# Seven products in the up layers, attention ahead, and a planned order, in an attention and two-layer kernel

## The chip, the cores and the metric

The kernel runs on one core of a Trainium2 chip. The metric is the time of one execution in microseconds, as the device takes it. PE is TensorE (matmuls), DVE is VectorE, ACT ScalarE, POOL GpSimd, SP SyncE, which here issues the DMAs.

## The reference, cut to what matters

Batch 2, 8 heads, 768 positions, head size 64; 1536 tokens of width 512; each layer goes to 2048 and back.

```python
for b in range(nb):                       # attention, by blocks of positions
    intra = np.einsum('bhic,bhjc->bhij', qb, kb) * Dmask[None]
    intra = np.einsum('bhij,bhjd->bhid', intra, vb)
    inter = np.einsum('bhid,bhde->bhie', qb * lam_pow[None], kv_state)
    out[:, :, sl] = intra + inter
    kv_state = lam_block[None, :, None, None] * kv_state + np.einsum('bhsd,bhse->bhde', kb_dec, vb)
x = attn_out.transpose(0, 2, 1, 3).reshape(1536, 512)
h = x @ w_in                              # layer 1: ELU
x = np.where(h > 0.0, h, np.exp(np.minimum(h, 0.0)) - 1.0) @ w_out
h = x @ moe2_w_in                         # layer 2: a slope of its own for each of 2048 columns
out = (np.maximum(h, 0.0) + alpha * np.minimum(h, 0.0)) @ moe2_w_out
```

## The kernel before

Every layer operand is held as two float32r tiles, a high half (a rounded copy, ACT) and a low half (the rest, a subtraction on POOL or DVE), and every product is three matmuls: high by high, high by low, low by high. The weights arrive as 64-bit words; `split_w` makes them float32 by one ACT pass (L125) and three DVE passes (L126, L128, L131) over 128x1024 tiles, and then splits them (L134 on ACT, L135 on POOL).

The tokens lie in three chunks of 512. An item is one chunk and one tile of 128 of the 2048 ff columns: `up` does twelve matmuls of 128x512 into a PSUM bank, ACT and DVE make `g` of it (L373 to L381), ACT and POOL split it (L383, L384), and two items later `down` does twelve matmuls. The four down sums of a chunk stay in PSUM for a group of four ff tiles, and then `flush` copies them to `acc` or adds them to it (L416). There are 96 items; the order is layer, group, chunk, ff tile.

Attention has twelve blocks of 128 positions. A block's work on PE is `state` (L223), `scores` of the next block (L201) and `outputs` (L256, L262); DVE masks the scores (L208), adds the state (L241) and takes the low half of the output (L275). Four blocks (`AHEAD`) run before the first item, the other eight each beside an item. The blocks of the second batch follow those of the first.

The order of every engine is that of the program. Work that belongs to a later place is put off by `later(n, step)`, which runs it after n ticks; a tick comes after every three up matmuls and after each down group. The numbers of ticks are written by hand (`gaps`, `first`, `early`, `when`). In `begin` the first weight load stands on the SP queue between the loads of the second and the third block. PSUM's eight banks are taken in turn by all.

Of the kernel before, what the change touches and what calls it, by code (L numbers as in the profile page):

```python
# [1 line left out]

# [20 lines left out]
NCH = NT // CH  # L23
NCC = DM // 128
NF = DFF // 128
NPAIR = NF // 2
NG = 4
GF = NF // NG
LAG = 2
AHEAD = 4  # L30
# [3 lines left out]
def attention_two_layers(  # L34
# [14 lines left out]
    PSUM = bass.MemoryType.PSUM  # L49


    tiny = ctx.enter_context(tc.tile_pool(name="tiny", bufs=1))
    const = ctx.enter_context(tc.tile_pool(name="const", bufs=1))
    wraw = ctx.enter_context(tc.tile_pool(name="wraw", bufs=3))
    wt = ctx.enter_context(tc.tile_pool(name="wt", bufs=2))

    wsp = ctx.enter_context(tc.tile_pool(name="wsp", bufs=3))

    accp = ctx.enter_context(tc.tile_pool(name="accp", bufs=4))
    small = ctx.enter_context(tc.tile_pool(name="small", bufs=2))  # L60
    tmp = ctx.enter_context(tc.tile_pool(name="tmp", bufs=2))
    gp = ctx.enter_context(tc.tile_pool(name="gp", bufs=LAG + 2))
    ps = ctx.enter_context(tc.tile_pool(name="ps", bufs=8, space=PSUM))

    def bank(name):
        return ps.tile([128, 512], F32, tag="ps", name=name)

    alpha_sb = tiny.tile([128, NF], F32, name="alpha_sb")
    beta = tiny.tile([128, NF], F32, name="beta")
    warm = tiny.tile([128, C], F32, name="warm")  # L70
    anti = tiny.tile([128, C], F32, name="anti")
    lam_sb = tiny.tile([128, H], F32, name="lam_sb")
    lamp = tiny.tile([128, H], F32, name="lamp")
    row = tiny.tile([1, 128 + H], F32, name="row")
    fill = tiny.tile([128, 40], F32, name="fill")


    clock = [0]
    due = {}

    def later(n, step):
        if n:
            due.setdefault(clock[0] + n, []).append(step)
        else:
            step()

    def tick():
        clock[0] += 1
        for step in due.pop(clock[0], []):
            step()  # L90
# [3 lines left out]
    raw = {}  # L94
    split = {}

    def load_w(c):
        n, part = divmod(c, 2)
        l, k = divmod(n, NPAIR)
        wi, wo = wts[l]  # L100
        r = wraw.tile([128, 2048], U32, tag="raw", name="raw")
        if part == 0:
            nc.sync.dma_start(
                out=r.rearrange("p (c f) -> p c f", c=NCC),
                in_=wi[:, k * 512:(k + 1) * 512].rearrange("(c p) f -> p c f", p=128))
        else:
            nc.sync.dma_start(
                out=r.rearrange("p (f e) -> p f e", f=2),
                in_=wo[k * 256:(k + 1) * 256, :].rearrange("(f p) e -> p f e", p=128))
        raw[c] = r  # L110

    def split_w(c, gaps=(5, 6, 8, 11, 13), first=3):
        n, part = divmod(c, 2)
        r = raw.pop(c).rearrange("p (f w) -> p f w", w=2)


        upper, lower = r[:, :, 1], r[:, :, 0]
        t = wt.tile([128, 1024], F32, tag="wt", name="wt")
        tu = t.bitcast(U32)
        tag = "wi" if part == 0 else "wo"  # L120
        h = wsp.tile([128, 1024], F32R, tag=tag + "h", name=tag + "h")
        lo = wsp.tile([128, 1024], F32R, tag=tag + "l", name=tag + "l")
        shape = dict(c=NCC) if part == 0 else dict(c=2)
        split[c] = [x.rearrange("p (c f) -> p c f", **shape) for x in (h, lo)]
        later(first, lambda: nc.scalar.mul(t, upper.bitcast(F32), 2.0 ** -112))  # L125
        later(gaps[0], lambda: nc.vector.tensor_scalar(  # L126
            out=tu, in0=tu, scalar1=3, scalar2=None, op0=ALU.logical_shift_left))
        later(gaps[1], lambda: nc.vector.scalar_tensor_tensor(  # L128
            out=tu, in0=lower, scalar=29, in1=tu,
            op0=ALU.logical_shift_right, op1=ALU.bitwise_or))  # L130
        later(gaps[2], lambda: nc.vector.scalar_tensor_tensor(  # L131
            out=tu, in0=upper, scalar=0x80000000, in1=tu,
            op0=ALU.bitwise_and, op1=ALU.bitwise_or))
        later(gaps[3], lambda: nc.scalar.copy(h, t))  # L134
        later(gaps[4], lambda: nc.gpsimd.tensor_tensor(  # L135
            out=lo, in0=t, in1=h.bitcast(F32), op=ALU.subtract))

    xh = {}
    xl = {}

    def new_x(t, nm):
        xh[t] = const.tile([128, NCC, CH], F32R, tag=f"xh{t}", name=f"{nm}h{t}")
        xl[t] = const.tile([128, NCC, CH], F32R, tag=f"xl{t}", name=f"{nm}l{t}")


    qp = small.tile([128, NP, C], F32, name="qp", bufs=1)
    lamc = qp[:, :, C - 1:C]
    dm = wsp.tile([128, 1024], F32, tag="wih", name="dm").rearrange(
        "p (s a i) -> p s a i", s=2, a=NP)

    rev = dm.rearrange("p s a i -> p a s i")[:, :, :, C - 1:C]
    sms = [wsp.tile([128, 1024], F32, tag=tag, name="sm").rearrange(
        "p (s a i) -> p s a i", s=2, a=NP) for tag in ("wil", "woh")]
    st2 = wsp.tile([128, 1024], F32, tag="wol", name="st").rearrange(
        "p (s a i) -> p s a i", s=2, a=NP)
    st = [st2[:, 0], st2[:, 1]]

    ld = {}
    vs = {}

    def load(n):


        t = accp.tile([128, 4, 512], F32, tag="acc", name="blk")
        z = t[:, 0:2].rearrange("p s (a i) -> p s a i", a=NP)
        nc.sync.dma_start(out=z, in_=kqT[n])
        m = 2 if n % PB != PB - 1 else 1
        u = t[:, 2:4].rearrange("p s (h d) -> p s h d", h=H)
        nc.sync.dma_start(
            out=u[:, 0:m], in_=vk[n, :, 0:m, :].rearrange("j a (h d) -> j a h d", h=H))  # L170
        ld[n] = z
        vs[n] = (u[:, 0], u[:, 1] if m > 1 else None)

    kd = {}
    qs = {}

    def scale(n):
        q_ = ld[n][:, 1]
        kk = vs[n][1]
        if kk is not None:  # L180
            kd_ = small.tile([128, H, D], F32, tag="kd", name="kd_t")
            nc.gpsimd.tensor_tensor(
                out=kd_.rearrange("p (a s) d -> p a s d", s=2),
                in0=kk.rearrange("p (a s) d -> p a s d", s=2),
                in1=rev.to_broadcast([128, NP, 2, D]), op=ALU.mult)
            kd[n] = kd_
        if n % PB:
            qs_ = small.tile([128, NP, C], F32, tag="qs", name="qs_t")
            nc.gpsimd.tensor_tensor(out=qs_, in0=q_, in1=qp, op=ALU.mult)
            qs[n] = qs_  # L190

    sc = {}

    def scores(n):
        z = ld[n]

        ps_ = [bank("sc"), bank("sc")]
        for pr in range(NP):
            for hs in range(2):
                a, b = hs * 64, (hs + 1) * 64  # L200
                nc.tensor.matmul(  # L201
                    out=ps_[hs][:, pr * C:(pr + 1) * C], lhsT=z[a:b, 0, pr, :],
                    rhs=z[a:b, 1, pr, :], start=True, stop=True)
        sc[n] = ps_

    def mask(n):
        for hs, p_ in enumerate(sc.pop(n)):
            nc.vector.tensor_tensor(  # L208
                out=sms[n % 2][:, hs], in0=p_.rearrange("p (a i) -> p a i", a=NP),
                in1=dm[:, hs], op=ALU.mult)  # L210

    cur = [0]

    def state(n):
        if n not in kd:
            return None
        kd_ = kd.pop(n)
        v_ = vs[n][0]
        p_ = bank("stp")
        for pr in range(NP):  # L220
            for hs in range(2):
                h = 2 * pr + hs
                nc.tensor.matmul(  # L223
                    out=p_[hs * 64:(hs + 1) * 64, pr * D:(pr + 1) * D], lhsT=kd_[:, h, :],
                    rhs=v_[:, h, :], start=pr == 0, stop=True, skip_group_check=True)
        return p_[:, 0:NP * D].rearrange("p (a d) -> p a d", a=NP)

    def new_state(n, p_):
        if p_ is None:
            return  # L230
        first = n % PB == 0
        old, new = st[cur[0]], st[1 - cur[0]]
        if not first:
            for pr in range(NP):
                nc.scalar.mul(new[:, pr, :], old[:, pr, :], lamc[:, pr, :])  # L235
        for hs in range(2):
            a, b = hs * 64, (hs + 1) * 64
            if first:
                nc.vector.tensor_copy(new[a:b, :, a:b], p_[a:b])
# [28 lines left out]
    def keep(n, po):  # L268
        t, o = divmod(n * C, CH)
        if o == 0:  # L270
            new_x(t, "x")
# [18 lines left out]
    def block_b(n, p_):  # L290
# [3 lines left out]
        if n + 4 < NBLK:  # L294
            load(n + 4)
# [246 lines left out]
```

## Time and profile before

| | |
|---|---|
| runs | 585.53, 585.78 (median), 586.66 us |
| profiled execution | span 584.1 us, from its first to its last instruction; its own time outside the span is not listed |
| instructions | 7319, of which PE has 2960 matmuls |
| DMA | 49.23 MB, mean 84 GB/s |

A span is the time between two instructions of one execution; the runs also hold what lies around it. The profile gives each engine's busy time, the chain of work that ended last, waits and who ended them, and a timeline of instructions.

### The profile page before, as it was taken

To read this page: it belongs to the slowest core of one execution; us is meant where nothing else is said; L and a number is where in the kernel's file an instruction comes from. 1 tells how busy PE (TensorE), PEld (TensorE's weight loads), DVE (VectorE), ACT (ScalarE), POOL (GpSimd) and SP (SyncE) were. 2 spreads that over 40 slices of the span, in tenths; PEclk is the share of its full clock that TensorE was granted. 3 is DMA by queue.
4 is the path that set the end of the run, shared out by engine and by line. 5 is a ranking of instruction groups with operands and counts; after the bars stand their busy time and mean duration, and the time that the engine had idled before them with its cause. 6 is when DMAs were issued, how large, how long until landed. Compare 5 with 4: busy or idle time off the path is not lost.

```text
span 584.1 us, 7319 instructions
## 1 busy us (share of the span) xinstructions
PE 575.3 (98%) x2960; PEld 475.6 (81%) x2960; DVE 271.8 (47%) x363; ACT 240.9 (41%) x374; POOL 227.9 (39%) x156
## 2 busy tenths in 40 slices
PE   7999999999999999999999999999999999999997
PEld 6886788888888888888888888888888888888886
DVE  7777444753534542543645731443553551641332
ACT  2536354565435444544654442533324323432220
POOL 3756512454324344344233444434415334432221
PEclk9999999999999999999999999999999999999999
DMA  8985300342202122122102212222204110000111
GB/s 323 412 329 172 101 1 6 140 143 73 73 0 85 60 73 72 73 72 73 53 20 81 68 69 73 72 74 72 73 0 141 31 46 0 2 0 1 72 73 72
DMA packets 18307, 49.23 MB, mean 84 GB/s; under 512 B 1250, under 2 KB 1506, under 8 KB 18274
## 3 DMA queue, kind: packets, MB, share of 16 engines
q1 hardware_dynamic: 18274, 48.77, 23.7%
q8 instruction: 23, 0.38, 0.3%
q14 instruction: 10, 0.08, 0.0%
HBM read 45.62 MB, written 3.15 MB: 83 GB/s over the span
## 4 chain that ended last, share of the span: by engine, by line
PE 93%; DVE 2%; DMA 2%; ACT 1%; POOL 0%; issue 0%; SPq 0%; DVEq 0%
PE dn L400 44%; PE up L362 43%; DMA raw<-in_w1i 2%; PE sc L201 1%; PE po L256 1%; PE po L262 1%; PE warm L281 1%; DVE wt L128 1%; PE stp L223 1%; ACT st L235 0%; DVE acc L416 0%; DVE wt L131 0%; POOL wol L135 0%; DVE st L241 0%; DVE wt L126 0%
## 5 line engine op out<-in xcount | busy, mean ns | idle before, releaser
L384 POOL TENSOR_TENSOR gl_t<-g_t,gh_t 128x512 fp32r<-128x512 f32 x96 | 125.1, 1304 | 320.4 <-ACT gh_t L383 265.9
L373 ACT ACTIVATE r_t<-up 128x512 f32<-128x512 f32 x96 | 57.3, 597 | 187.2 <-PE up L362 187.2
L383 ACT CAST gh_t<-g_t 128x512 fp32r<-128x512 f32 x96 | 59.6, 621 | 110.9 <-DVE g_t L377 57.9
L416 DVE TENSOR_TENSOR acc<-dn,acc 128x512 f32<-128x512 f32 (+1 forms) x73 | 46.9, 676 | 75.7 <-PE dn L400 75.7
L400 PE MATMUL dn<-gh_t,wol 128*128 128x512 f32 x192 | 74.9, 390 | 1.3 <-POOL wol L135 1.3
L381 DVE SCALAR_TENSOR_TENSOR g_t<-r_t,beta,up 128x512 f32<-128x512 f32 x48 | 35.7, 743 | 86.2 <-ACT r_t L373 77.5
L400 PE MATMUL dn<-woh,gl_t 128*128 128x512 f32 (+1 forms) x196 | 75.4, 385 | 0.0
L400 PE MATMUL dn<-woh,gh_t 128*128 128x512 f32 (+1 forms) x196 | 75.4, 385 | 0.0
L400 PE MATMUL dn<-wol,gh_t 128*128 128x512 f32 (+1 forms) x196 | 75.4, 385 | 0.0
L400 PE MATMUL dn<-gh_t,woh 128*128 128x512 f32 x192 | 75.3, 392 | 0.0
L400 PE MATMUL dn<-gl_t,woh 128*128 128x512 f32 x192 | 74.8, 389 | 0.0
L377 DVE SCALAR_TENSOR_TENSOR g_t<-r_t,up 128x512 f32<-128x512 f32 x48 | 32.8, 683 | 63.0 <-ACT r_t L376 63.0
L362 PE MATMUL up<-xh,wih 128*128 128x512 f32 x192 | 52.2, 394 | 0.0
L362 PE MATMUL up<-xl,wih 128*128 128x512 f32 x192 | 51.4, 389 | 0.0
L362 PE MATMUL up<-xh,wil 128*128 128x512 f32 x192 | 51.4, 389 | 0.0
L362 PE MATMUL up<-yh,wih 128*128 128x512 f32 x192 | 51.3, 389 | 0.0
L362 PE MATMUL up<-yl,wih 128*128 128x512 f32 x192 | 51.3, 389 | 0.0
L362 PE MATMUL up<-yh,wil 128*128 128x512 f32 x192 | 51.3, 389 | 0.0
L126 DVE TENSOR_SCALAR wt<-wt 128x1024 uint32<-128x1024 uint32 x32 | 29.7, 927 | 33.5 <-ACT wt L125 33.5
L400 PEld LDWEIGHTS dn<-gh_t,wol 128*128 128x128 f32 x192 | 36.0, 188 | 9.2 <-POOL wol L135 1.7
L400 PEld LDWEIGHTS dn<-woh,gl_t 128*128 128x128 f32 x196 | 36.8, 188 | 7.4
L400 PEld LDWEIGHTS dn<-wol,gh_t 128*128 128x128 f32 x196 | 36.8, 188 | 7.4
(57 smaller groups left out, 796.2 us busy)
## 6 DMA issues: line engine op xcount, KB each, us to landing
raw<-in_w1i SPq DMA_DIRECT2D x8, 1024.0 KB, 5.6
raw<-in_w1o SPq DMA_DIRECT2D x8, 1024.0 KB, 4.8
raw<-in_w2i SPq DMA_DIRECT2D x8, 1024.0 KB, 5.4
raw<-in_w2o SPq DMA_DIRECT2D x8, 1024.0 KB, 4.9
blk<-in_kqT SPq DMA_DIRECT2D x12, 512.0 KB, 6.9
blk<-in_vk SPq DMA_DIRECT2D x10, 512.0 KB, 8.2
out<-acc SPq DMA_DIRECT2D x11, 256.0 KB, 2.1
blk<-in_vk SPq DMA_DIRECT2D x2, 256.0 KB, 6.4
```

Of the source, the lines that this page charges most:

```text
L126: later(gaps[0], lambda: nc.vector.tensor_scalar(out=tu, in0=tu, scalar1=3, scalar2=None, op0=ALU.logical_shift_left))
L128: later(gaps[1], lambda: nc.vector.scalar_tensor_tensor(out=tu, in0=lower, scalar=29, in1=tu, op0=ALU.logical_shift_right, op1=ALU.bitwise ...
L201: nc.tensor.matmul(out=ps_[hs][:, pr * C:(pr + 1) * C], lhsT=z[a:b, 0, pr, :], rhs=z[a:b, 1, pr, :], start=True, stop=True)
L223: nc.tensor.matmul(out=p_[hs * 64:(hs + 1) * 64, pr * D:(pr + 1) * D], lhsT=kd_[:, h, :], rhs=v_[:, h, :], start=pr == 0, stop=True, skip_ ...
L362: nc.tensor.matmul(out=p_, lhsT=w[:, cc, fo:fo + 128], rhs=x[t][:, cc, :], start=n == 0, stop=n == 3 * NCC - 1)
L373: nc.scalar.activation(r, p_, AF.Relu, scale=-1.0)
L377: later(1, lambda: nc.vector.scalar_tensor_tensor(out=g, in0=r, scalar=-1.0, in1=p_, op0=ALU.add, op1=ALU.max))
L381: later(1, lambda: nc.vector.scalar_tensor_tensor(out=g, in0=r, scalar=beta[:, f:f + 1], in1=p_, op0=ALU.mult, op1=ALU.add))
L383: later(2, lambda: nc.scalar.copy(gh_, g))
L384: later(3, lambda: nc.gpsimd.tensor_tensor(out=gl_, in0=g, in1=gh_.bitcast(F32), op=ALU.subtract))
L400: nc.tensor.matmul(out=p_, lhsT=a, rhs=b, start=first and n == 0, stop=last and n == 2)
L416: nc.vector.tensor_tensor(out=a, in0=p_, in1=a, op=ALU.add)
```

## The change

Chunk 0 keeps its plain up products (`plain`). For chunks 1 and 2 and a pair of ff tiles the up product is a 2 by 2 block product (two ff tiles, two halves of the 512 inputs, two chunks of tokens), done as Strassen's seven products in Winograd's form (`PRODUCTS`, `seven`). The weight sums S1 to S4 are made for each pair (`weights`, `sums`), the token sums T1 to T4 once a layer (`combine`), in place in the `acc` tiles of chunks 1 and 2. Three partial results are copied out of PSUM (`kept`), three are added to them on DVE (`tile`), one goes to its nonlinearity from PSUM.

A down sum now takes only one pair of ff tiles in PSUM (six matmuls); every pair's is added to `acc`. The PSUM banks are given out by use: 0 to 2 to the seven products, 3 and 4 to plain ones, 5 to 7 to down sums.

All twelve attention blocks run before the layers, the two batches in turn (`ORDER`); the state is updated in place. The first weight loads wait for the outputs of the blocks in places 2 and 5 (`W0`, `W1`), and no weight load stands among the first block loads.

`build` states each operation with its cost per engine, what it reads and what it writes, and PE's order. `Plan.run`, a list scheduler that runs while the program is written, then gives each other engine its order: of what is ready, what PE needs first. It may give an operation to ACT or DVE, or to DVE or POOL, and keeps operations marked `shared` of DVE and POOL apart in its plan. On the chip the engines run in that order and wait for one another as before.

The core of the diff; of the removed lines only the items and the PSUM groups of before are shown.

```diff
+ORDER = [b * PB + k for k in range(PB) for b in range(B)]
+CHUNK = [[0, 6, 1, 7], [2, 3, 4, 5], [8, 9, 10, 11]]
...
+    def add(self, costs, run, reads=(), writes=(), late=0.0, shared=False):
+        op = Op(costs, run, late, shared)
+        for b in reads:
+            op.after.update(b.wrote)
+        for b in writes:
+            op.after.update(b.read or b.wrote)
+        for b in reads:
+            b.read.append(op)
+        for b in writes:
+            b.wrote, b.read = [op], []
+        op.after.discard(op)
+        self.ops.append(op)
+        return op
...
+                held = []
+                while ready[e]:
+                    item = heapq.heappop(ready[e])
+                    op = item[2]
+                    if op.begun:
+                        continue
+                    if op.shared and e in port and port[self.OTHER[e]] > now + 1e-9:
+                        held.append(item)
+                        continue
+                    if e == "POOL" and any(
+                            x.shared and not x.begun and x is not op and x.need < op.need
+                            and x.need + shift < now + op.costs[e] + self.HOLD for _, _, x in ready["DVE"]):
+                        held.append(item)
+                        continue
+                    slow = op.costs[e] - op.least
+                    slack = op.need + shift - now
+                    if slow > 0.3 and slack < slow or (
+                            e == "DVE" and "POOL" in op.costs and slack > self.SPARE) or (
+                            e == "DVE" and "ACT" in op.costs and slack > self.EASE):
+                        held.append(item)
+                        continue
+                    begin(e, op)
+                    break
+                for item in held:
+                    heapq.heappush(ready[e], item)
...
+def act(n, psum=False):
+    return ((172 if psum else 224) + n) / 1200
+def vec(n):
+    return (140 + n) / 960
+def vec2(n):
+    return (150 + n / 2) / 960
+def pool(n):
+    return 0.2 + n * 0.00214
...
+    def sub(dst, a, b, reads, writes, n, engines=("DVE", "POOL"), alu=ALU.subtract):
+        costs = {"DVE": vec(n), "POOL": pool(n)}
+        op({e: costs[e] for e in engines},
+           lambda e: on(e).tensor_tensor(out=dst(), in0=a(), in1=b(), op=alu),
+           reads, writes, shared=True)
...
+        eng = ("DVE", "POOL")
+        sub(lambda: s1, lambda: a21, lambda: a22, [b_t], [b_y], 256, eng, ALU.add)
+        sub(lambda: s3, lambda: a11, lambda: a21, [b_t, b_y], [b_y], 256, eng)
+        sub(lambda: s2, lambda: s1, lambda: a11, [b_t, b_y], [b_y], 256, eng)
+        sub(lambda: s4, lambda: a12, lambda: s2, [b_t, b_y], [b_y], 256, eng)
+        held[l, j] = y, b_y
...
+            p11, p21, p12, p22 = (place(raw1, 0), place(raw1, 1), place(raw2, 0), place(raw2, 1))
+            q11, q21, q12, q22 = (bufs(raw1, 0), bufs(raw1, 1), bufs(raw2, 0), bufs(raw2, 1))
+            if l:
+                parts("B11", p11, q11)
+            sub(p11, p12, p11, q11 + q12, q11, 2 * n)
+            parts("T1", p11, q11)
+            if l:
+                parts("B22", p22, q22)
+            sub(p12, p22, p12, q12 + q22, q12, 2 * n)
+            sub(p22, p22, p11, q11 + q22, q22, 2 * n)
+            parts("T2", p22, q22)
+            parts("T3", p12, q12)
+            if l:
+                parts("B21", p21, q21)
+            sub(p21, p21, p22, q21 + q22, q21, 2 * n)
+            parts("T4", p21, q21)
...
+    W0, W1 = 2, 5
...
+    PRODUCTS = [
+        ("A11", "B11", 0, 1, 0), ("A12", "B21", 1, 1, 1), ("S1", "T1", 2, 1, 0),
+        ("S2", "T2", 0, 0, 0), ("S4", "B22", 2, 0, 1), ("S3", "T3", 0, 0, 0),
+        ("A22", "T4", 0, 0, 1)]
...
+    def seven(l, j):
+        s = j % 2
+        for n, (a, b, k, opens, closes) in enumerate(PRODUCTS):
+            k = (k + j) % 3
+            def run(a=a, b=b, k=k, opens=opens, closes=closes):
+                i = 0
+                for w, x in ((0, 0), (0, 1), (1, 0)):
+                    for cc in range(2):
+                        nc.tensor.matmul(
+                            out=banks[k], lhsT=left(s, a, w)[:, cc, :],
+                            rhs=quad(b, x)[:, cc, :], start=bool(opens and i == 0),
+                            stop=bool(closes and i == 5), skip_group_check=True)
+                        i += 1
+            reads = [b_quad[b, p, o] for p in range(2) for o in range(2)]
+            reads += b_wa[s] if a[0] == "A" else b_ws
+            yield pe(6 * MM, run, reads, [b_ps[k]])
+            def kept(u, k=k):
+                copy(lambda: ut(u), lambda: banks[k], [b_ps[k]], [b_ut[u]], 512, True)
+            def tile(u, q, t, k=k):
+                op({"DVE": vec(512)}, lambda e: nc.vector.tensor_tensor(
+                    out=ut(u), in0=banks[k], in1=ut(u), op=ALU.add),
+                   [b_ps[k], b_ut[u]], [b_ut[u]])
+                finish(l, 2 * j + q, lambda: ut(u), b_ut[u], (l, j, q, t), False)
+            if b == "B11":
+                kept(0)
+            elif b == "B21":
+                tile(0, 0, 1)
+            elif b == "T1":
+                kept(1)
+            elif b == "T2":
+                kept(2)
+            elif b == "B22":
+                tile(2, 0, 2)
+            elif b == "T3":
+                tile(1, 1, 2)
+            else:
+                finish(l, 2 * j + 1, lambda k=k: banks[k], b_ps[k], (l, j, 1, 1), True)
...
+        for c in range(parts):
+            k = 5 + turn("dn", 3)
+            cols = slice(c * w, (c + 1) * w)
+            p_ = banks[k][:, 0:w]
+            def run(cols=cols, p_=p_):
+                i = 0
+                for q in range(2):
+                    g = gt(gslot[l, j, q, t])
+                    for a, x in ((0, 0), (0, 1), (1, 0)):
+                        if l == 0:
+                            lhs, rhs = wd(s, a)[:, q, e * 128:(e + 1) * 128], g[:, x]
+                        else:
+                            lhs, rhs = g[:, x, e * 128:(e + 1) * 128], wd(s, a)[:, q, cols]
+                        nc.tensor.matmul(
+                            out=p_, lhsT=lhs, rhs=rhs, start=i == 0, stop=i == 5)
+                        i += 1
+            reads = [b_g[gslot[l, j, q, t]] for q in range(2)] + b_wd[s]
+            yield pe(6 * MM / parts, run, reads, [b_ps[k]])
...
+            if j == 0:
+                copy(a, lambda p_=p_: p_, [b_ps[k]], b_a, 512, True)
+            else:
+                op({"DVE": vec(w)}, lambda _, a=a, p_=p_: nc.vector.tensor_tensor(
+                    out=a(), in0=p_, in1=a(), op=ALU.add), [b_ps[k], *b_a], b_a)
...
+    T0 = [(0, e) for e in range(4)]
+    T12 = [(t, e) for t in (2, 1) for e in range(4)]
+    E12 = [(t, e) for e in range(4) for t in (2, 1)]
...
+        for i in range(4):
+            block_load(i)
         scores(0)
         scale(0)
         scale(1)
+        for i in range(NBLK):
+            k = state(i)
+            if i + 1 < NBLK:
+                scores(i + 1)
+            outputs(i)
+            new_state(i, k)
+            if i + 4 < NBLK:
+                block_load(i + 4)
+            if i + 2 < NBLK:
+                scale(i + 2)
+            if i == 5:
+                b_raw[0].wrote, b_raw[1].wrote = [last[W0]], [last[W1]]
+                weights(0, 0)
+                sums(0, 0)
+                weights_down(0, 0)
...
+        for l in range(2):
             if l == 0:
+                merge(plain(0, 0))
+                weights(0, 1)
+                weights_down(0, 1)
+                merge(plain(0, 1))
+                merge(seven(0, 0), downs(0, 0, T0))
             else:
+                merge((), downs(1, 0, T0))
+                merge(seven(1, 0), downs(1, 1, T0))
+            sums(l, 1)
+            for j in range(1, NU - 1):
+                merge(chain(seven(l, j), at_once(weights, l, j + 1), at_once(sums, l, j + 1),
+                            plain(l, j + 1)),
+                      chain(*([downs(l, j, T0), downs(l, j - 1, T12)] if (l, j) == (0, 1) else
+                              [downs(l, j - 1, T12)]), at_once(weights_down, l, j + 1),
+                            downs(l, j, T0) if j > 1 else ()))
+            j = NU - 1
+            merge(seven(l, j), chain(downs(l, j, T0), downs(l, j - 1, T12)))
+            if l == 1:
+                merge((), downs(1, j, T12))
...
+            weights(1, 0)
+            sums(1, 0)
+            weights_down(1, 0)
+            weights(1, 1)
+            merge(chain(plain(1, 0), plain(1, 1)), downs(0, j, E12))
+            raw = [(acc[t], {(e, q): b_acc[t, e, q] for e in range(4) for q in range(2)})
+                   for t in (1, 2)]
+            combine(1, 1, *raw)
+            weights_down(1, 1)
...
-    items = [(l, q, t, q * GF + j)
-             for l in range(2) for q in range(NG) for t in range(NCH) for j in range(GF)]
-    PER = NCH * GF
...
-        if first:
-            dn[e, c0] = bank("dn")[:, 0:c1 - c0]
```

## Rows read from the trace of the kernel before

**Rows 1.** The page: engine, busy us, share, instructions.

```profile
PE 575.3 (98%) x2960; PEld 475.6 (81%) x2960; DVE 271.8 (47%) x363; ACT 240.9 (41%) x374; POOL 227.9 (39%) x156
```

**Rows 2.** The chain in time: start us, us, what.

```profile
98.80 2.72 PE dn L400 x12
...
316.40 2.72 PE dn L400 x12
```

**Rows 3.** Waits of PE: total us, times, longest us.

```profile
PE sc L201 <- DMA blk<-in_kqT: 2.3, 1, 2.3
PE dn L400 <- POOL wol L135: 1.3, 1, 1.3
...
PE po L262 <- DVE st L241: 0.5, 1, 0.5
```

**Rows 4.** Windows: busy us by engine, PE clock, DMA share, GB/s.

```profile
10.00:15.00 5.00, 2.73 (x44) 2.52 (x42) 4.01 (x7) 1.71 (x2) 1.95 (x3) 0.89 1.04 416
15.00:20.00 5.00, 5.00 (x62) 4.30 (x60) 3.20 (x4) 1.47 (x3) 4.95 (x4) 0.77 1.03 409
```

**Rows 5.** Groups by line: busy us, mean ns, idle before.

```profile
L384 POOL TENSOR_TENSOR gl_t<-g_t,gh_t 128x512 fp32r<-128x512 f32 x96 | 125.1, 1304 | 320.4 <-ACT gh_t L383 265.9 <-PE dn L400 52.6 <-PE up L362 1.8
...
L416 DVE TENSOR_TENSOR acc<-dn,acc 128x512 f32<-128x512 f32 x71 | 46.2, 683 | 75.7 <-PE dn L400 75.7
L128 DVE SCALAR_TENSOR_TENSOR wt<-raw,wt 128x1024 uint32<-128x1024 uint32 x32 | 40.7, 1270 | 1.0
...
L135 POOL TENSOR_TENSOR wol<-wt,woh 128x1024 fp32r<-128x1024 f32 x16 | 38.4, 2399 | 2.3 <-ACT woh L134 2.3
...
L126 DVE TENSOR_SCALAR wt<-wt 128x1024 uint32<-128x1024 uint32 x32 | 29.7, 927 | 33.5 <-ACT wt L125 33.5
...
L411 ACT COPY acc<-dn 128x512 f32<-128x512 f32 x12 | 7.0, 581 | 2.9 <-PE dn L400 2.1 <-POOL qs_t L189 0.7
```

**Rows 6.** Timeline near 40 us: start, us, engine, what.

```profile
39.47 1.96 DVE L128 SCALAR_TENSOR_TENSOR wt<-raw,wt 128x1024 uint32<-128x1024 uint32 x1
...
40.31 2.27 POOL L189 TENSOR_TENSOR qs_t<-blk,qp 128x512 f32<-128x512 f32 x1
```

**Rows 7.** Timeline near 150 us.

```profile
149.76 1.88 DVE L416 TENSOR_TENSOR acc<-dn,acc 128x512 f32<-128x512 f32 x3
...
150.58 1.30 POOL L384 TENSOR_TENSOR gl_t<-g_t,gh_t 128x512 fp32r<-128x512 f32 x1 [4.15 <-ACT gh_t L383]
```

**Rows 8.** Timeline of the end.

```profile
578.21 0.40 PE L400 MATMUL dn<-woh,gh_t 128*128 128x512 f32 x1
...
578.40 2.73 DVE L416 TENSOR_TENSOR acc<-dn,acc 128x512 f32<-128x512 f32 x5 [4.72 <-PE dn L400]
...
580.17 0.28 PE L400 MATMUL dn<-wol,gh_t 128*128 128x256 f32 x1
```

**Rows 9.** Timeline of PE in attention, two stretches.

```profile
10.72 0.69 PE L223 MATMUL stp<-blk,kd_t 128*64 128x64 f32 x16
...
24.58 1.09 PE L256 MATMUL po<-sm,blk 128*64 128x128 f32 x16
...
28.40 1.20 PE L362 MATMUL up<-xh,wih 128*128 128x512 f32 x4
```

**Rows 10.** The page: DMA issues, KB each, us to landing.

```profile
raw<-in_w1i SPq DMA_DIRECT2D x8, 1024.0 KB, 5.6
```

**Rows 11.** Timeline of DVE in attention, one block.

```profile
22.31 1.28 DVE L208 TENSOR_TENSOR sm<-sc,dm 128x512 f32<-128x512 f32 x2
23.50 0.85 DVE L241 TENSOR_TENSOR st<-stp,st 64x256 f32<-64x256 f32 x2
24.38 0.69 DVE L275 TENSOR_TENSOR xl<-po,xh 128x512 fp32r<-128x512 f32 x1
```

**Rows 12.** Timeline of DVE, the last scans of the start.

```profile
6.38 2.16 DVE L335 TENSOR_TENSOR_SCAN qp<-lamp,warm 128x128 f32<-128x128 f32 x4
```

More of the change, by code (lines that the diff above doesn't have):

```diff
@@ L73, in attention_two_layers @@
[L73 to L83, printed above, removed]
-        else:
[L85 to L90, printed above, removed]
-    wts = [(w1i, w1o), (w2i, w2o)]
[L94 to L105, printed above, removed]
-        else:
[L107 to L136, printed above, removed]
@@ L192, in attention_two_layers, with on, sb @@
[L192 to L198, printed above, removed]
+    mem = ctx.enter_context(tc.tile_pool(name="mem", bufs=1))
+    psum = ctx.enter_context(tc.tile_pool(name="psum", bufs=1, space=bass.MemoryType.PSUM))
+    plan = Plan()
+    def on(e):
+        return {"ACT": nc.scalar, "DVE": nc.vector, "POOL": nc.gpsimd}[e]
+    def sb(name, shape, dt=F32, tag=None):
+        return mem.tile([128, *shape], dt, tag=tag or name, name=name)
@@ new lines, in attention_two_layers, with turn, pe, op @@
+    b_ut = [Buf() for _ in range(3)]
+    b_rt = [Buf() for _ in range(3)]
+    b_ps = [Buf() for _ in range(8)]
+    turns = {}
+    def turn(name, n):
+        turns[name] = turns.get(name, -1) + 1
+        return turns[name] % n
+    def pe(cost, run, reads, writes):
+        return plan.add({"PE": cost}, lambda e: run(), reads, writes)
+    def op(costs, run, reads, writes, shared=False):
+        return plan.add(costs, run, reads, writes, 0.0, shared)
+    def load(out_, in_, mb, writes):
+        plan.add({"SP": 0.05}, lambda e: nc.sync.dma_start(out=out_, in_=in_), (), writes,
+                 late=mb / 0.36)
@@ L212, in attention_two_layers @@
[L212 to L237, printed above, removed]
-            if first:
-                nc.vector.tensor_copy(new[a:b, :, a:b], p_[a:b])
-            else:
-                nc.vector.tensor_tensor(
-                    out=new[a:b, :, a:b], in0=p_[a:b], in1=new[a:b, :, a:b],
-                    op=ALU.add)
-        cur[0] = 1 - cur[0]
@@ L328, in begin, with masks @@
+                nc.vector.tensor_copy(
+                    lamp[a:b, 0:NP], lam_sb.rearrange("p (a s) -> p s a", s=2)[a:b, hs])
+        op({"DVE": 0.34}, halves, [b_lam], [b_lamp])
+        def masks(e, hs):
             for pr in range(NP):
@@ new lines, in attention_two_layers, with merge, chain, downs @@
+    b_y0 = [[Buf() for _ in range(4)] for _ in range(2)]
+    def merge(up, dn=()):
+        up, dn = iter(up), iter(dn)
+        while True:
+            a, b = next(up, None), next(dn, None)
+            if a is None and b is None:
+                return
+    def chain(*steps):
+        for s in steps:
+            yield from s
+    def downs(l, j, ts):
+        for t, e in ts:
+            yield from down(l, j, t, e, 2 if (l, j, t, e) == (1, NU - 1, 1, 3) else 1)
+            if e == 3:
+                gfree.extend(gslot[l, j, q, t] for q in range(2))
@@ L495, with at_once @@
+    def at_once(step, *args):
+        step(*args)
+        return
+        yield
+    build()
+    with tc.manual_schedule():
+        plan.run()
 def kernel(**inputs):
```

803 lines of the change are left out of this document (523 added, 280 removed).

## Prediction

> **What bounds the kernel now.** I read the page's busy times first: PE is busy for 575.3 of 584.1 us, and DVE, ACT and POOL for less than half of it [rows 1]. Busy PE time is modelled, so the chain in order of time comes next. From about 98 us to the end it is nothing but groups of twelve L362 or L400 matmuls; between the two pieces shown there are 80 groups in 217.6 us, 2.72 us each [rows 2]. One 512-column matmul thus costs 226.7 ns, whether it is an up or a down product. The layers have 1152 of each (96 items of twelve up and twelve down matmuls), 2304 x 0.2267 = 522.3 us. PE is the bound, and its order is fixed. The other 61.8 us are the start, attention and the tail.
>
> Where does PE lose time there? It waits 2.3 us for the keys of the third block, 1.3 us for the low half of a down weight, 0.5 us for the state [rows 3]. Around the first of these the granted clock falls to 0.89 and then 0.77 of 2.4 GHz, so part of ten microseconds ran at the 1.2 GHz level after PE had idled [rows 4]: 5 x 0.11 + 5 x 0.23 = 1.7 us, of which I count 1.5, since some of the slow stretch was idle anyway.
>
> The sum is made against the span of the profiled execution, 584.1 us; its own time outside the span is not listed. The runs shown lie 1.4 to 2.6 us above the span and their median 1.7; I add that 1.7 at the end.
>
> **The change, part by part.**
>
> *Products.* A pair of ff tiles (call it a step; there are eight a layer) needed 2 x 2 x 12 = 48 up matmuls for two chunks. Seven products of six are 42. Chunk 0 keeps its 24, down its 72. Six fewer, 16 steps: 96 x 0.2267 = **21.8 us less** on the engine that sets the end. Weight, moving and output shapes stay 128x128 and 128x512. A step is now 138 x 0.2267 = 31.3 us of PE.
>
> *Extra work per step on the other engines.* Down sums were kept in PSUM over four ff tiles and added to `acc` then; now every step adds all twelve. DVE per step: 12 adds, 3 adds of the kept products and 6 ELUs at 0.683 (their PSUM source and size are those of L416; in layer 1 a little longer), 14.3 us; two conversions at 0.927 + 1.270 + about 1.27 us, 6.9 us; together 21.2 of 31.3 us [rows 5]. POOL, if it takes all that may lie on it: six low halves at 1.304, three 1024-wide ones at 2.399, four weight sums of 256 columns, priced at half of 1.304 (bounds: a quarter to all of it): 17.6 us [rows 5]. ACT: what it did before, 240.9 us, plus 48 kept products at 0.581, the time of its copy out of PSUM [rows 5], and 16 more 1024-wide high halves at up to twice that, 46 us: 287, half of the span. So all three fit under PE. What hides them is a whole step of slack for weights and most of a step for g; without that cover 21.2 us of DVE a step would be 339 us on the path. PE doesn't wait for throughput, only for short slacks.
>
> *Port between DVE and POOL.* A conversion took 1.96 us, not 1.27, while POOL worked, and the POOL instruction beside it 2.27 us [rows 6]; three adds that read PSUM went at 0.6 us apiece beside an undisturbed 1.30 us of POOL [rows 7]. So some kinds exclude each other, and adds from PSUM don't. Of a step's DVE work the conversions and three ELUs whose inputs are both in SBUF can clash: 8.9 us, with POOL 26.5 of 31.3. The Trainium skill (SBUF — State Buffer, Who interferes with whom) calls it an exclusive lock for a whole instruction, taken by a DVE instruction with two SBUF inputs or in a two-port mode. By that rule the clashing work queues up to those 26.5 us, still below 31.3, and the sum is the same; by a free overlap it would be 21.2. The trace agrees with the kinds.
>
> *Shortest slack.* Bank 0 takes products A11B11, S2T2, S3T3 and A22T4 of a step in turn. A22T4 may not start before DVE has added the S3T3 state, and between the two lies one down group, 1.36 us. Handing over takes 0.19 us (578.21 to 578.40) [rows 8] each way, the add 0.683: 0.30 us are to spare. Behind A22T4 all of PE waits. If DVE is idle it costs 0; if it has just begun a 1.27 us instruction, 0.97 us, 15.5 in 16 steps. DVE is busy two thirds of the time, mostly with 0.683 us instructions, of which on average half is left, about the spare: I take **+2 us**. The kept copies of the other products have 4.1 us and don't count.
>
> *Attention first.* All twelve blocks now run before the first up product; only the place of the work changes. A block in full flow takes PE 3.8 us (24.58 to 28.40) [rows 9]. The first weight load (1 MB [rows 10], SP queue) no longer stands ahead of blocks 2 and 3 but follows block 2's output: at 416 GB/s [rows 4] they land 2.5 us earlier, so the 2.3 us gap after the state products of 10.72 us [rows 9] closes, and with it the slow clock: **-3.8 us**. Later loads, 1 MB a block, take 2.5 us against 3.8 of PE, and the two delayed weight loads go into that slack. The waits of 1.3 and 0.5 us were from interleaving: **-1.8 us**, or nothing back at worst.
>
> *What the front must now do.* Between blocks DVE has 1.28 + 0.85 + 0.69 = 2.8 us a block [rows 11], 34 us for twelve. Before the second plain product of the first layer (two groups of 24 matmuls, 5.4 us each, follow attention) it needs also three conversions and a low half, 11.5 us: 45.5 us, between 8.5 us, when the scans end [rows 12], and about 56 us. That leaves 2 us of 47.5. If the gaps fill, the cost is 0; if DVE idles for a sixth of the attention as it waits for PE, ACT and state, 8 us. I take the middle, **+4 us**. The combining of chunks 1 and 2 then has 16 us until T1 is needed and its chain is some 4 us; it is late only if DVE is.
>
> *Layer border.* After the last down of layer 0 PE has four down groups and two of up and down, 8.2 us, until B21, and 13.6 us until T2. Their chains are one add, a high half, a low half (up to 2.4 us on POOL), 4 us, and for T2 three more DVE passes at 1.27 and a second split, 9 us. They have to share DVE with conversions: 0 to 5, taken **+1.5 us**. At the end the last down group is halved as before; the 3.9 us from its last matmul at 580.17 [rows 8] stay.
>
> Sum: 584.1 - 21.8 - 3.8 - 1.8 + 2 + 4 + 1.5 = 564.2 us of span, 565.9 with what lies around it; I say **566 us**.
>
> **The rivals.**
> 1. *No new stall.* The source's planner puts the urgent instruction first, and its costs (0.68 for an add, 1.30 for a POOL half) are those of the trace [rows 5], so its order can be right. 584.1 - 27.4 + 1.7 = 558.4 us. Against it: the front is full to 2 us.
> 2. *Late DVE.* The slack at A22T4 goes in two steps of three (16 x 0.65 = 10 us), the front costs 6, the border 3: 584.1 - 27.4 + 19 + 1.7 = 577 us. For it: DVE's busy time rises from 271.8 us to 16 x 21.2 + 34 for attention + some 20 for start and combining = 393, 70% of the span, in one fixed order.
> 3. *Slower: the add stuck behind a locked port.* A DVE conversion waits for POOL's 1024-wide half, and the add that frees bank 0 stands behind it in DVE's queue. Late by 2.4 - 0.3 = 2.1 us a step it costs 34 us: 584.1 - 27.4 + 34 + 1.7 = 592 us. It decides from 27.4 / 16 = 1.7 us of PE stall in every step. For it: there is such a pair [rows 6]. Against: POOL runs only three such halves in 31 us, so every step would have to meet the same pair; and that pair lost 0.7 us on DVE and 1.0 on POOL, which in every step would be 11 to 16 us, rival 2. The lock that the same page of the Trainium skill states would let the loser wait out the whole instruction, the 592; no row shows so long a wait.
> 4. *The change doesn't save the matmuls' time* because PE waits at the seven products anyway, within 0.2%: the point between 2 and 3, 586 us.
>
> **How the numbers follow.** Forecast (561 to 570 us) 0.55, rival 1 (below 561) 0.13, rival 2 (570 to 584) 0.21, rival 4 0.03, rival 3 0.08. The range takes the forecast, the nearer half of rival 1 and most of rival 2: 558 to 579 us. Faster by over 0.2%, which is about what a measurement here can tell: 0.55 + 0.13 + 0.21 = 0.89; same 0.03; slower 0.08.
>
> **What would show it.** Right: 2208 layer matmuls; a chain of six-matmul groups at 1.36 us through all steps; first up product near 50 us; clock 1.0 from 10 to 20 us; DVE some 390 us busy; PE's waits summing to less than 10 us, on DVE at the A22T4 line once a step and on weights near 55 us. Wrong: PE waits of over half a microsecond in each step, on DVE or POOL; a front that ends after 60 us; a slow clock; or matmuls above 227 ns.

## Result and profile after

The changed kernel takes 565.17 us in the median (564.93 to 569.97) against 586.22 before, a ratio of 0.966 with a 95% interval of 0.962 to 0.969. Forecast were 566 us, within 558 to 579. Two later sets gave 566.13 (ratio 0.967, 0.964 to 0.970) and 566.19 us (0.965, 0.963 to 0.967). The profiled execution took 564.93 us, with a span of 563.0 us.

The page, to be read against [rows 1], then PE's waits in the whole trace (total, times, longest), against [rows 3]:

```profile
PE 551.8 (98%) x2858; PEld 457.0 (81%) x2858; DVE 415.4 (74%) x550; ACT 292.4 (52%) x460; POOL 295.5 (52%) x205
```

```profile
PE ps L751 <- DVE step L764: 3.0, 2, 2.2
PE ps L719 <- DVE step L689: 1.3, 1, 1.3
PE ps L800 <- DVE g L344: 1.2, 2, 0.8
PE ps L473 <- DVE warm L617: 1.1, 1, 1.1
PE ps L530 <- POOL kdqs L503: 1.0, 1, 1.0
PE ps L555 <- DVE smqp L491: 0.5, 2, 0.4
```

PE is still the bound. DVE went from 271.8 to 415.4 us of work, and PE's waits, on DVE and POOL, are few: eight besides the start (`warm`), 7.0 us together. Now the front, in windows against [rows 4] and in PE's timeline against [rows 9], and the last matmul:

```profile
10.00:15.00 5.00, 5.00 (x92) 4.44 (x86) 4.89 (x12) 1.17 (x2) 3.23 (x3) 1.00 1.02 404
15.00:20.00 5.00, 4.48 (x62) 3.75 (x62) 3.75 (x9) 1.75 (x5) 2.56 (x4) 1.00 1.01 380
```

```profile
10.40 0.64 PE L530 MATMUL ps<-blk,kdqs 128*64 128x64 f32 x16
10.96 1.16 PE L486 MATMUL ps<-blk 64*128 64x128 f32 x16
...
51.40 1.17 PE L719 MATMUL ps<-x0h,wah 128*128 128x512 f32 x4
...
559.66 0.28 PE L800 MATMUL ps<-wdl,g 128*128 128x256 f32 x1
```

The third block's scores follow at 10.96 us without a gap, the clock stays at full speed, and the layers start at 51.40 us. From there to the end of the last matmul (559.66 + 0.12) are 508.4 us; 2208 x 0.2267 = 500.5 us are matmuls, so the layers lose 7.9 us. Before, 580.29 - 522.3 = 58.0 us of PE's time were not layer matmuls. So the span changed by -21.8 (matmuls), -6.6 (58.0 to 51.4), +7.9 (waits in the layers) and -0.6 (tail, 3.8 to 3.2 us): -21.1 us, as 584.1 to 563.0.

**Where the 7.9 us lie.** Five places make 7.2 us of it, each wait counted with the slower start behind it: the second plain pair (L719, 1.6 us), step 0 of layer 1 (2.4) and of layer 2 (1.05), and two down groups, one at the end of layer 1 (1.0) and one at the start of layer 2 (1.1). The largest is in step 0 of layer 1 (the bank that A22T4 needs):

```profile
76.23 0.62 PE L751 MATMUL ps<-qT3h,wsh 128*128 128x512 f32 x2
...
76.91 1.28 POOL L344 TENSOR_TENSOR g<-step,g 128x512 fp32r<-128x512 f32 x1 [0.44 <-ACT g L336]
77.11 2.16 DVE L378 SCALAR_TENSOR_TENSOR wt<-raw,wt 128x1024 uint32<-128x1024 uint32 x1
...
79.19 0.68 DVE L764 TENSOR_TENSOR step<-ps,step 128x512 f32<-128x512 f32 x1
...
79.93 0.73 PE L751 MATMUL ps<-qT4h,wah 128*128 128x512 f32 x2 [2.17 <-DVE step L764]
```

S3T3 ends near 77.6 us. The add that must read its bank (L764) stands in DVE's queue behind a conversion, and the conversion, begun 0.2 us after a POOL instruction, took 2.16 us and not the 1.2 of an undisturbed one. Nothing lies on PE between S3T3 and A22T4 here: the first step of a layer has four down groups for seven products. In a later step the same three instructions look so:

```profile
158.49 0.62 PE L751 MATMUL ps<-qT3h,wsl 128*128 128x512 f32 x2
...
158.94 0.61 PE L800 MATMUL ps<-g,wdh 128*128 128x512 f32 x2
159.16 0.68 DVE L764 TENSOR_TENSOR step<-ps,step 128x512 f32<-128x512 f32 x1
...
160.31 0.61 PE L751 MATMUL ps<-qT4h,wah 128*128 128x512 f32 x2
```

The add ends at 159.84 us, the down group at 160.31, and PE doesn't wait. In 13 of the 14 covered steps A22T4 follows within 0.01 us; in one it is 0.06 us late. Near the end of layer 1 a down group waits:

```profile
269.30 2.39 POOL L344 TENSOR_TENSOR wal<-wt,wah 128x1024 fp32r<-128x1024 f32 x1
...
269.91 2.33 DVE L344 TENSOR_TENSOR g<-step,g 128x512 fp32r<-128x512 f32 x1
...
272.29 0.50 PE L800 MATMUL ps<-g,wdh 128*128 128x512 f32 x1 [0.76 <-DVE g L344]
```

A low half that takes 0.68 us elsewhere took 2.33, and ended 0.55 us after POOL's instruction had ended at 271.69. The groups by line, against [rows 5], show what such clashes add up to: the conversions' last two passes 1.46 and 1.40 us in the mean, and POOL's halves of `g` 1.51 where they were 1.30; an add out of PSUM is as it was.

```profile
L811 DVE TENSOR_TENSOR acc<-ps,acc 128x512 f32<-128x512 f32 x167 | 114.9, 689 | 91.9 <-PE ps L800 91.1
L344 POOL TENSOR_TENSOR g<-step,g 128x512 fp32r<-128x512 f32 x71 | 106.8, 1509 | 112.5 <-ACT g L336 112.3
...
L378 DVE SCALAR_TENSOR_TENSOR wt<-raw,wt 128x1024 uint32<-128x1024 uint32 x32 | 46.7, 1462 | 0.0
```

### The profile page after: what moved, and what is told of

Its sections match the earlier page's. It is cut to its first block, busy times and chain, and to the rows that moved or that the text cites. A ratio compares the mean times of both kernels' runs of the same rounds, so it can differ in the third digit from the quotient of the medians.

```text
span 563.0 us, 7427 instructions
## 1 busy us (share of the span) xinstructions
PE 551.8 (98%) x2858; PEld 457.0 (81%) x2858; DVE 415.4 (74%) x550; ACT 292.4 (52%) x460; POOL 295.5 (52%) x205
## 4 chain that ended last, share of the span: by engine, by line
PE 93%; DVE 4%; ACT 1%; issue 1%; POOL 0%; DVEq 0%; POOLq 0%
PE ps L800 46%; PE ps L751 26%; PE ps L719 15%; PE ps L486 2%; PE ps L555 1%; PE ps L561 1%; PE ps L530 1%; PE ps L473 1%; DVE wt L378 1%; DVE g L344 1%; DVE smqp L491 0%; DVE wsl L344 0%; ACT wt L370 0%; DVE step L764 0%; DVE smqp L654 0%
## 5 line engine op out<-in xcount | busy, mean ns | idle before, releaser
L811 DVE TENSOR_TENSOR acc<-ps,acc 128x512 f32<-128x512 f32 (+1 forms) x169 | 115.8, 686 | 92.2 <-PE ps L800 91.4
L344 POOL TENSOR_TENSOR g<-step,g 128x512 fp32r<-128x512 f32 x71 | 106.8, 1509 | 112.5 <-ACT g L336 112.3
L800 PE MATMUL ps<-wdh,g 128*128 128x512 f32 (+1 forms) x388 | 118.9, 387 | 0.5 <-DVE g L344 0.4
L800 PE MATMUL ps<-g,wdh 128*128 128x512 f32 x384 | 118.5, 389 | 0.8 <-DVE g L344 0.8
L800 PEld LDWEIGHTS ps<-wdh,g 128*128 128x128 f32 x388 | 72.6, 188 | 16.1 <-DVE g L344 0.8
L800 PEld LDWEIGHTS ps<-g,wdh 128*128 128x128 f32 x384 | 72.1, 188 | 16.1 <-DVE g L344 1.2
L800 PE MATMUL ps<-wdl,g 128*128 128x512 f32 (+1 forms) x194 | 75.1, 387 | 0.0
L336 ACT CAST g<-step 128x512 fp32r<-128x512 f32 x94 | 57.9, 620 | 32.9 <-DVE step L689 16.5
L800 PE MATMUL ps<-g,wdl 128*128 128x512 f32 x192 | 74.7, 389 | 0.0
L378 DVE SCALAR_TENSOR_TENSOR wt<-raw,wt 128x1024 uint32<-128x1024 uint32 x32 | 46.7, 1462 | 0.0
L764 DVE TENSOR_TENSOR step<-ps,step 128x512 f32<-128x512 f32 x48 | 33.0, 688 | 18.2 <-PE ps L751 17.3
L375 DVE SCALAR_TENSOR_TENSOR wt<-raw,wt 128x1024 uint32<-128x1024 uint32 x32 | 44.8, 1400 | 0.2
L344 POOL TENSOR_TENSOR wdl<-wt,wdh 128x1024 fp32r<-128x1024 f32 x12 | 31.7, 2639 | 21.1 <-ACT wdh L336 21.1
L719 PE MATMUL ps<-x0l,wah 128*128 128x512 f32 x128 | 38.6, 389 | 0.0
```

Source lines behind the costliest of these rows:

```text
L336: nc.scalar.copy(dst(), src())
L344: lambda e: on(e).tensor_tensor(out=dst(), in0=a(), in1=b(), op=alu),
L375: op({"DVE": vec(1024)}, lambda e: nc.vector.scalar_tensor_tensor(out=tu, in0=lower, scalar=29, in1=tu, op0=ALU.logical_shift_right, op1=A ...
L378: op({"DVE": vec(1024)}, lambda e: nc.vector.scalar_tensor_tensor(out=tu, in0=upper, scalar=0x80000000, in1=tu, op0=ALU.bitwise_and, op1=A ...
L719: nc.tensor.matmul(out=banks[k], lhsT=wa[s][w][:, cc, q * 128:(q + 1) * 128], rhs=x0[x][:, cc, :], start=i == 0, stop=i == 11)
L764: op({"DVE": vec(512)}, lambda e: nc.vector.tensor_tensor(out=ut(u), in0=banks[k], in1=ut(u), op=ALU.add), [b_ps[k], b_ut[u]], [b_ut[u]])
```

## Experiments

The theory: the matmuls give 21.8 us; the front gives some 6; waits at a few places without cover take 6 to 8 back. Each expectation has a rival that says the gain or the loss lies elsewhere. Notes behind # in the cuts of code are not in the kernels.

**Plain products in the new order** (`e1_plain_up`).

```diff
-        for n, (a, b, k, opens, closes) in enumerate(PRODUCTS):
+        for t in (2, 1):
+            for q in range(2):       # twelve matmuls, read from PSUM by finish()
...
-            sub(p11, p12, p11, q11 + q12, q11, 2 * n)   # and all other sums of tokens and weights
```

> Chunks 1 and 2 get plain up products again (48 matmuls a step, four tiles read from PSUM, no weight or token sums, no kept products); attention first, the planner, the banks and the down sums stay as in the changed kernel. Theory (the matmul count made the gain): 96 x 0.2267 = 21.8 us come back, less up to 3 us for the two waits at A22T4 that can't occur: 584 to 587 us. Rival (the order of attention and the planner made most of it): under 575 us.

580.94 us (ratio 0.990, 0.988 to 0.992). Neither: it lies 15.8 us above the changed kernel's first set and 14.8 above its second (566.13). PE's timeline, first and last layer matmuls:

```profile
51.70 1.18 PE L695 MATMUL ps<-x0h,wah 128*128 128x512 f32 x4
...
575.73 0.28 PE L754 MATMUL ps<-wdl,g 128*128 128x256 f32 x1
```

The layers run from 51.70 to 575.85 us, 524.2, of which 2304 x 0.2267 = 522.3 are matmuls: it loses 1.9 us there, not 7.9. Both profiled executions ran at a granted clock of 1.0. So the layers differ by 524.2 - 508.4 = 15.8 us: the seven products save 21.8 and lose 6.0 more in waits than plain products do. The other parts of the change together are worth 586.88 - 580.94 = 5.9 us by themselves. The expectation allowed 3 us for the waits, too little. DVE has 343.3 us of work here: half of its rise from 271.8 to 415.4 comes with the seven products, half with the rest of the change.

**The load order alone, in the kernel before** (`e2_before_wload`).

```diff
         load(1)
-        load_w(0)
         load(2)
         load(3)
+        load_w(0)
```

> The kernel before, with its first weight load behind the loads of blocks 2 and 3. Theory: the 2.3 us wait for the third block's keys and the slow clock after it go, 3.8 us: 581.5 to 583.5 us. Rival (the time is set there by the weights, whose conversion comes later by as much as the blocks come sooner): no gain, 585.5 to 586.5 us.

592.36 us (1.009, 1.008 to 1.011): slower by 5.5 us, and both guesses are wrong. DVE's timeline, then PE's in the same stretch, then windows:

```profile
19.12 0.69 DVE L126 TENSOR_SCALAR wt<-wt 128x1024 uint32<-128x1024 uint32 x1 [6.70 <-ACT wt L125]
19.84 1.23 DVE L128 SCALAR_TENSOR_TENSOR wt<-raw,wt 128x1024 uint32<-128x1024 uint32 x1
20.99 1.28 DVE L208 TENSOR_TENSOR sm<-sc,dm 128x512 f32<-128x512 f32 x2
```

```profile
15.08 1.16 PE L201 MATMUL sc<-blk 64*128 64x128 f32 x16
21.73 2.56 PE L256 MATMUL po<-sm,blk 128*64 128x128 f32 x16 [5.48 <-DVE sm L208]
```

```profile
20.00:25.00 5.00, 2.56 (x16) 1.85 (x16) 3.40 (x4) 1.57 (x4) 0.45 (x1) 0.56 1.01 406
25.00:30.00 5.00, 3.29 (x26) 2.98 (x28) 4.07 (x8) 3.61 (x10) 4.02 (x3) 0.50 0.64 229
```

The 2.3 us gap is gone, but the conversion stands ahead of a block's masks in DVE's order. It waits for the later weights, the masks (L208) wait behind it, and PE for the masks; then PE runs at 1.2 GHz for most of ten microseconds (mean granted clock 0.56 and 0.50 of 2.4 GHz in the two windows). So the load may move only together with the conversion's place on DVE and ACT, which the changed kernel does.

**No cover in any step** (`e4_no_cover`).

```diff
-            yield pe(6 * MM, run, reads, [b_ps[k]])
+            pe(6 * MM, run, reads, [b_ps[k]])
+            if b != "T3":
+                yield 1
```

> The changed kernel with A22T4 directly behind S3T3 in every step; the down group that lay between them follows A22T4. Theory (only that down group hides the add that frees the bank): each of 14 steps waits 1.0 to 1.5 us, as the two uncovered first steps of a layer do (2.2 and 0.8 us): 579 to 586 us. Rival (the two waits came from a backlog on DVE at the start of a layer, not from the missing cover): under 569 us.

582.36 us (0.993, 0.990 to 0.995), as the theory has it. PE's waits at that product, all of them:

```profile
PE ps L751 <- DVE step L766: 14.8, 16, 2.2
```

In 13 of 16 steps the wait is 0.78 or 0.79 us, and A22T4 comes 0.94 or 0.95 us late. So it is the add and two hand-overs, with DVE ready: 0.20 us from the product's end to the add, 0.69 for the add, 0.06 from its end to A22T4. In the other three DVE was busy. The cover, not DVE's load, keeps the 14 steps free.

**First come, first served** (`e5_fifo`).

```diff
-                    heapq.heappush(ready[e], (op.need, n, op))
+                    heapq.heappush(ready[e], (n, n, op))
```

> The changed kernel, whose planner takes what became ready first in place of what PE needs first. Theory (short slacks need the order): conversions and low halves stand ahead of the adds, over 10 us lost: above 575 us. Rival (DVE and POOL have room enough, any order that never idles does): under 568 us.

579.29 us (0.988, 0.985 to 0.990). The size is right, the reason isn't:

```profile
PE ps L719 <- DVE wah L338: 12.0, 1, 12.0
...
PE ps L751 <- DVE step L764: 1.6, 2, 0.8
```

One wait, before the second plain pair, near 60 us, makes nearly all of it, and the 1.2 GHz stretch behind it: DVE had worked through token sums, conversions and low halves that were needed later. In the steps no more is lost than in the changed kernel (1.6 us at A22T4, there 3.0). What the order by need buys is the front, where 45.5 of 47.5 us of DVE were spoken for.

**A plan that doesn't know of the port** (`e7_no_port`).

```diff
-                    if op.shared and e in port and port[self.OTHER[e]] > now + 1e-9:
-                        held.append(item)
-                        continue
...
-                    if e == "POOL" and any(
```

> The changed kernel, whose planner no longer keeps DVE and POOL apart where both need their common port. Theory (an instruction that finds the port taken waits for the other's end, so a plan that doesn't know of it is late): over 3 us more than the changed kernel. Rival (the chip queues the two by itself at no loss): within 1.5 us of it.

584.11 us (0.995, 0.994 to 0.997), 18 us above the changed kernel on the same chip: nearly all of the gain. The waits are spread; the two longest groups, and one conversion pass by its group:

```profile
PE ps L711 <- DVE step L681: 6.8, 1, 6.8
PE ps L743 <- DVE step L756: 4.6, 4, 2.6
```

```profile
L370 DVE SCALAR_TENSOR_TENSOR wt<-raw,wt 128x1024 uint32<-128x1024 uint32 x32 | 62.3, 1951 | 0.3
```

That pass took 1462 ns in the changed kernel. Of DVE's instructions, 40 take over 0.9 us longer than the shortest of their kind, against 15 in the changed kernel and 2 in the one before. The longest wait, 6.8 us, is again that of the second plain pair, near 66 us.

**Mending the waits by a new order of PE** (`e3_cover_first`, `e6_three_waits`, `e8_four_waits`), beside the changed kernel (`after_again`, 566.13 us).

```diff
-                merge(seven(0, 0), downs(0, 0, T0))
+                merge(seven(0, 0), downs(0, 0, T0), (4, 5))   # no down group behind products 4 and 5
...
+            k = (2, 7)[q] if (l, j) == (0, 1) else 3 + turn("up", 2)                 # e6, e8
+            merge(seven(l, j), chain(downs(l, j - 1, T12[:4]), downs(l, j, T0), ...  # e6, e8
+                            downs(l, j, T0) if j > 1 else ()), (1, 2) if (l, j) == (1, 1) else ())   # e8
```

> The changed kernel once more, beside the kernels that follow, on their chip: 564.5 to 566 us.

> The changed kernel; in the first step of each layer, which has only four down groups for seven products, the fourth lies between S3T3 and A22T4 in place of behind S2T2. Theory (the missing cover makes those two waits of 2.2 and 0.8 us): 2 to 3.3 us less than the changed kernel, 561.9 to 563.2 us. Rival (DVE is late there anyway, and the wait moves to another product): less than 0.5 us.

> As the run with the cover in the first steps, and two more edits: the second plain pair of layer 1 gets banks 2 and 7, so that it needn't wait until DVE has read bank 3 (1.4 us with its restart), and in the last step of a layer four down groups of the step before go ahead of chunk 0's, whose low half was late (1.0 us). Theory (each wait has its own local cause): 4.4 to 5.7 us less than the changed kernel, 559.5 to 561 us. Rival (DVE is simply full there and the waits move): less than 3 us.

> As the run with three waits mended, and in step 1 of layer 2 two up products go first, so that the low half for its first down group is ready (1.1 us lost with its restarts). Theory: another 0.8 to 1.1 us, 558.6 to 560.2 us. Rival (the down groups pile up behind and wait there for their bank): no gain.

573.25 (0.979, 0.977 to 0.981), 575.03 (0.981, 0.979 to 0.983) and 574.72 us (0.979, 0.977 to 0.981): all slower than the changed kernel by 7 to 9 us. PE's waits with the first edit alone:

```profile
PE ps L751 <- DVE step L689: 3.1, 1, 3.1
PE ps L800 <- DVE wdh L338: 2.3, 1, 2.3
...
PE ps L800 <- DVE wdl L344: 1.5, 1, 1.5
```

The waits at A22T4 are gone, but others stand elsewhere, one ahead of S1T1 in step 1 and two for the down weights at the start of layer 2. The edit of PE's order changed the plan of every other engine too. The theory of local causes isn't refuted by this, nor shown; the next two runs keep the plan.

**The same waits with the plan kept** (`e9_put_off`, `e10_put_off_3`), beside the changed kernel (`after_third`, 566.19 us). The planner runs as before; a marked instruction group is only issued behind PE's next one.

```diff
+            if op.defer:
+                put_off.append(op)
+            else:
+                op.run(e)
+                if e == "PE":
+                    while put_off:
+                        put_off.pop().run(e)
...
+            x.defer = b == "T4" and j == 0                                      # e9, e10
+            x.defer = e == 0 and (l, j, t) in ((0, NU - 1, 0), (1, 0, 2))       # e10
```

> The changed kernel, beside the three kernels that follow, on their chip: 564.5 to 566.5 us.

> The plan is made as before, and every other engine keeps its order to the instruction; only on PE, A22T4 of each layer's first step is put behind the first product of the next step. Theory (the two waits of 2.2 and 0.8 us come from the missing cover, and the slower runs with the cover came from a new plan): 1.8 to 2.5 us less than the changed kernel. Rival (the cover moves the wait to the next product whatever the plan): less than 0.5 us.

> As the run with A22T4 put off, and in the same way the first down group of chunk 0 in the last step of layer 1 and the first one of step 0's other chunks in layer 2 go behind the next up product; each had waited for its low half. Theory: another 1.4 to 2.0 us, in all 3.2 to 4.5 us less than the changed kernel, 560.5 to 563 us. Rival (the adds behind them on DVE come later and hold up their banks): no further gain.

564.35 (0.963, 0.961 to 0.965) and **562.67 us** (0.959, 0.958 to 0.961), against 0.965 (0.963 to 0.967) of the changed kernel beside them. By the medians that is 1.8 and 3.5 us less, but two of the four executions of the changed kernel beside them ran at a mean granted clock of 0.997. Executions at 1.0 took 564.2 to 564.5 us with the first edit and 562.5 to 562.7 with all three, against 564.8 and 565.7: some 0.9 and 2.6 us less. The second gain is clear; the first is smaller than forecast, and its interval overlaps that of the changed kernel. PE's waits in the layers, first with A22T4 put off alone, then with all three:

```profile
PE ps L809 <- DVE g L345: 1.2, 1, 1.2
...
PE ps L758 <- DVE step L773: 0.8, 1, 0.8
```

```profile
PE ps L726 <- DVE step L696: 1.3, 1, 1.3
PE ps L758 <- DVE step L773: 1.2, 2, 0.8
```

With one product as cover, the wait of 2.2 us in layer 1 became 0.8; the conversion behind which the add stands still takes 2.17 us. In layer 2 the wait of 0.8 at A22T4 went, but the next down group then waited 1.2 us for its high half, where it had waited 0.1. So the cover alone moved part of the wait, as its rival said; the third edit took that too. This is the fastest version here, with the same matmuls.

## Why the prediction was right, point by point

- *Products, 21.8 us.* Right as a gross sum: undoing them costs 15.8 in the layers, and the 6.0 between is the difference of the losses there, 7.9 and 1.9.
- *Other engines fit under PE.* Right for this plan. DVE came to 415 us where 393 were forecast. Conversions took 1.46 and 1.40 where 1.27 was assumed, and ELUs with both inputs in SBUF 0.91 where 0.683 was, some 21 us in all; DVE also did 38 us of low halves of `g` and of weights that the forecast gave to POOL. Other items came to less than forecast. That the port would change nothing in the sum was too simple: a plan blind to it costs 18 us.
- *Shortest slack, +2 us.* The size was about right (2.3 + 0.95 us late), the place wrong. It was spread over 16 steps with a busy DVE; the 14 covered steps lose next to nothing, and the two first steps, which have no down group between S3T3 and A22T4, lose it all. The step that failed is "between the two lies one down group": it was not counted in each step. The price without cover, 0.19 + 0.683 + 0.19 = 1.06 us, measured 0.95, as the second hand-over took 0.06; the spare of a covered step is thus about 0.4 us, not 0.30.
- *Attention first, -3.8 and -1.8 us.* PE's time outside the layers fell by 6.6 us, with 1.5 us of new waits in it, so 8.1 came where 5.6 were forecast. The waits and the slow clock named there are gone. But the reason given for the 3.8, a weight load that stands later in its queue, does not give it alone; there it costs 5.5. The other 2.5 us were put at nothing ("only the place of the work changes"). The trace of before has a loss of that size:

```profile
61.51 1.20 PE L362 MATMUL up<-xh,wih 128*128 128x512 f32 x4
62.55 1.08 PE L362 MATMUL up<-xh,wil 128*128 128x512 f32 x4
63.47 1.08 PE L362 MATMUL up<-xl,wih 128*128 128x512 f32 x4
64.47 1.09 PE L256 MATMUL po<-sm,blk 128*64 128x128 f32 x16
```

  The four matmuls behind attention take 1.04 us from start to start (61.51 to 62.55), the four ahead of it 1.00 (63.47 to 64.47), others 0.91. Before, PE changed 25 times between the two, which lengthened layer products by 2.8 us in all; now it changes once. That is read from the traces; no run took it by itself.
- *Front, +4 us.* 1.5 us of waits in attention (in other executions of the same kernel 2.7 to 2.9) and 1.4 us before the second plain pair: 2.9. The latter isn't the wait for weights that was forecast near 55 us: PE waits until DVE has read a bank (L689), and that ELU stands behind a conversion in DVE's queue.
- *Border, +1.5 us.* Two places, 2.1 us with restarts, but neither waits for the combining of tokens, whose price was worked out; they wait for low halves of g.
- *Rival 3*, the instruction stuck behind a locked port, is real, and the argument against it was too weak: no row chosen for it shows so long a wait, but the trace of before has two, near 104 and 112 us (below). Afterwards PE waits behind such an instruction at two places, not in every step. That the 18 us of the blind plan are all of this kind was not taken apart.
- *The sum.* That 566 lies within 1 us of the result is in part luck. In us of the span, attention gave 2.5 more than forecast, the front cost 1.1 less and the tail 0.6 less; A22T4 cost 1.3 more and the border 0.6 more, and 1.1 of smaller losses stood in no term.

What stays open: why the plans of the three re-ordered kernels put the down weights late. Each was run once in that form, and the planner's choice was not taken apart.

## What to carry to other kernels

On an engine that is always busy, fewer instructions count in full, but their dependences come with them: look for each place where an accumulator is read and written again, and count what lies between on that engine, above all in the first and last turns of a loop, where the filler is missing. Move a load only with all that waits for it in the queues. Where a planner orders the work, mend a wait by moving the one instruction behind the plan, and look where the wait goes; a new input to the plan is a new kernel.

## What the runs showed of the hardware

A DVE instruction with both inputs in SBUF, started 0.6 us into a POOL instruction of 2.39 us, ended 0.55 us after POOL's end: 2.33 us in place of 0.68. This is what the Trainium skill (SBUF — State Buffer, Who interferes with whom) states, a lock for a whole instruction. The trace of before had it too, with a conversion pass that takes 0.68 us at its shortest and here ended 0.55 us after POOL's end:

```profile
111.60 2.41 POOL L135 TENSOR_TENSOR wol<-wt,woh 128x1024 fp32r<-128x1024 f32 x1
...
112.28 2.28 DVE L126 TENSOR_SCALAR wt<-wt 128x1024 uint32<-128x1024 uint32 x1 [2.07 <-ACT wt L125]
```

The same wait of 2.2 us at 80 us was followed by full speed in one profiled execution of the changed kernel and by 1.2 GHz in another (a window of `after`, then two of `after_third`; the clock is the number behind the last bracket):

```profile
82.00:84.00 2.00, 2.00 (x11) 1.65 (x10) 1.95 (x3) 1.01 (x2) 0.00 (x0) 1.00 0.78 322
...
82.00:84.00 2.00, 2.00 (x6) 1.53 (x5) 2.00 (x4) 0.74 (x2) 0.00 (x0) 0.50 0.96 381
84.00:86.00 2.00, 2.00 (x7) 1.61 (x6) 0.92 (x1) 0.47 (x1) 0.00 (x0) 0.65 0.30 123
```

The two slow windows cost 2 x 0.50 = 1.0 and 2 x 0.35 = 0.7 us; of the 2.6 us between the two profiled spans the other 1.0 is a longer wait in attention. The changed kernel's executions with a mean clock of 1.0 took 564.8 to 565.7 us, those with 0.997 and 0.994 took 566.7 to 570.0 us, so most of its spread goes with the clock; the slowest were not profiled.
